# Turning the first of four token pairs by VectorE blocks and DRAM instead of TensorE

## The chip, the cores and the metric

The kernel runs on one core of a Trainium2 chip. The metric is the device time of one execution in microseconds, as a median over several runs. A profiled execution comes with it, in which every instruction of every engine has a start and a duration.

## The reference, cut to what matters

All data are fp32. There are 2048 tokens of 576 features; the two-part layer below is applied twice.

```python
def _A_ref(x, dft_seq_re, dft_seq_im, dft_hid_re, dft_hid_im):
    a = jnp.einsum("bsd,ed->bse", x, dft_hid_re)
    b = jnp.einsum("bsd,ed->bse", x, dft_hid_im)
    y = jnp.einsum("ts,bse->bte", dft_seq_re, a) - jnp.einsum("ts,bse->bte", dft_seq_im, b)
    return y
def _B_ref(x, w1, b1, w2, b2):
    y = _layernorm(x, axis=-1)
    h = _gelu(jnp.einsum("bsd,df->bsf", y, w1) + b1)          # 576 -> 4608
    return jnp.einsum("bsf,fd->bsd", h, w2) + b2              # 4608 -> 576
x = A_x
for _ in range(2):
    x = x + _A_ref(_layernorm(x, axis=-1), ...)
    x = x + _B_ref(_layernorm(x, axis=-1), ...)
```

## The kernel before

Every fp32 product is made of three TensorE passes over two parts of each operand: a high part, rounded to fp32r by ScalarE, and a low part, which is the rest and which VectorE gets by subtracting. The large products are cut into two by two blocks and done with seven block products instead of eight, so block sums of each operand are needed too, and each of the seven operands needs its high and its low part.

A layer has a sequence stage (DFT over tokens), and then, for each half of the 1024 tokens, a *feature phase* (`hidden`, DFT over features, residual, layer norm) and the channel MLP (`mlp`). So there are four feature phases in an execution. The change touches only them.

A feature phase goes through eight tiles of 128 tokens, n = 0 to 7. Tiles 2j and 2j+1 form *pair* j; one comes from the first 512 tokens of the half and one from the second. For tile n, `hidden` does in this order:

- SyncE loads operands two tiles ahead (`h.load(n + 2)`, four DMAs from `uv_mid` and one for the residual).
- `turn(n + 1)` splits the next tile's left operand (ScalarE high, L201; VectorE low, 128x1152).
- `next(ln)` lets the previous tile's layer norm go on: `normalize` (ScalarE, L252) writes the normalized tile n-1 into the pair's block `t8[j]`.
- `rests(j)` (ScalarE, L922), at even n, copies the 32 features that don't fill a block of 128.
- 54 matmuls of 288 columns into a PSUM pair from `space()`, a ring of four.
- in the middle of these (k = 2 of 9), at n = 3 and 5, `turn_sums` makes high and low parts of two single blocks and one more (through `parts`), and then four block differences on VectorE (128x384 each). At k = 4 GpSimd adds the output bias to the residual tile.
- after the matmuls, VectorE adds the result to the residual tile (L195) and makes the statistics of tile n (`stats`: VectorE, then three small GpSimd instructions, L229 to L233).
- at n = 3 and 5, `turn_parts` makes the parts of the four sums (one ScalarE instruction of 1536 elements, two VectorE ones).
- at n = 2, 4 and 6, `turn_blocks(n // 2 - 1)` turns pair j = 0, 1, 2: eight TensorE transposes of 128x128 (L936), four of 96 columns (L939), and two ScalarE copies from PSUM (L940, L941). Pair 3 has a path of its own at the end.

The operand `y` of the MLP has tokens along its free dimension, which is why the normalized tiles are turned at all. The order of instructions on each engine is the order in which the program writes them (`manual_schedule`); an engine doesn't pass an instruction that waits. Two blocks of 2304 columns (`t8s`) hold the pairs in turn: pair 0 and pair 2 have the same one. Nearly all vector and DMA instructions go through helpers, so their lines in the profile are those of the helpers: L192 `dma`, L195 `add`, L198 `sub`, L208 `mm`.

Of the kernel before, what the change touches and what calls it, by code (L numbers as in the profile page):

```python
# [8 lines left out]
F32 = mybir.dt.float32  # L9
F32R = mybir.dt.float32r  # L10
AF = mybir.ActivationFunctionType
# [4 lines left out]
P = 128  # L16
NT = S // P
DH = D // 2
NP = NT // 2
# [138 lines left out]
def spectral_mixer(ctx: ExitStack, tc: tile.TileContext, x, dh, c0, cs, w1, b1, w2, b2, out):  # L158
# [8 lines left out]
    nc = tc.nc  # L167
# [23 lines left out]
    def dma(dst, src):  # L191
        nc.sync.dma_start(dst, src)  # L192

    def add(engine, dst, a, b, op=OP.add):
        engine.tensor_tensor(dst, a, b, op=op)  # L195

    def sub(engine, dst, a, b):
        engine.tensor_tensor(dst, a, b, op=OP.subtract)  # L198

    def split(hi, lo, src):  # L200
        nc.scalar.activation(hi, src, AF.Copy)  # L201
        sub(nc.vector, lo, src, hi.bitcast(F32))
# [4 lines left out]
    def mm(o, a, b, start, stop):  # L207
        nc.tensor.matmul(o, a, b, start=start, stop=stop, skip_group_check=True)  # L208


    def moments():

        t = small.tile([P, 34], F32, name="moments")
        return (t[:, :24].rearrange("p (a b) -> p a b", a=2),
                t[:, 24:].rearrange("p (a b) -> p a b", a=2))

    def stats(src, twice=False, plain=False):


        st, mv = (v[:, 0] for v in moments())  # L220
# [12 lines left out]
        nc.gpsimd.tensor_tensor(mv[:, 4:5], power[:, 2:3], mv[:, 4:5], op=OP.subtract)  # L233
        return mv
# [16 lines left out]
    def normalize(dst, src, mv):  # L251
        nc.scalar.activation(dst, src, AF.Identity, bias=mv[:, 4:5], scale=mv[:, 3:4])  # L252
# [3 lines left out]
    stage, raw = R.alloc(3 * 5 * P, low=True), A.alloc(4 * 3 * P, low=True)  # L256
# [493 lines left out]
    class Hidden:  # L750
# [106 lines left out]
        def turn(self, n, place=None):  # L857
            if n >= NP:
                return
            v = self.uv[n](2 * D)  # L860
            v = (v.bitcast(F32) if self.half else v).rearrange("p (q k t) -> p k q t", q=4, t=32)
            self.ut[n] = place or R.place(UT_AT[self.half][n % 2], 2 * KH * P)
            o = self.ut[n](2, KH, 4, 32)
            split(o[:, 0], o[:, 1], v)
            yield
            self.uvs.give(self.uv.pop(n))

    def drain(*gens):
        gens = list(gens)
        while gens:  # L870
            for g in list(gens):
                if next(g, "end") == "end":
                    gens.remove(g)

    def hidden(h, mlp):

        half, src, order, turn = h.half, h.src, h.order, h.turn
        ring = None

        def space():  # L880
            return pp[ring.pop(0)] if ring else h.space()
# [6 lines left out]
        y = Y(7, 5, TC)  # L888
        t8s = Slots(A, 2, 8 * DH)
        es, b2t = A.alloc(7 * 3 * 32, low=True), A.alloc(D, low=True)  # L890
        dma(b2t(D), b2.to_broadcast([P, D]))
        t8 = {}

        def norms(n):

            if n % 2 == 0:
                t8[n // 2] = t8s.take()
            v = t8[n // 2](8, DH)
            tile_x = xv[:, :, order[n]]
# [4 lines left out]
            if n < NP - 1:  # L904
# [12 lines left out]
            yield  # L917

        def rests(j):
            v = t8[j](8, DH)  # L920
            if j < 3:
                nc.scalar.activation(es(7, 3, 32)[:, :4], v[:, 0:4, None, 2 * P:].to_broadcast([P, 4, 3, 32]), AF.Copy)  # L922
                return
            e = es(7, 3, 32)
            nc.scalar.activation(e[:, :, 1].bitcast(F32R), v[:, 1:8, 2 * P:], AF.Copy)  # L925
            nc.gpsimd.tensor_copy(e[:, :, 0], v[:, 1:8, 2 * P:])
            sub(nc.gpsimd, e[:, :, 2], v[:, 1:8, 2 * P:], e[:, :, 1])
# [12 lines left out]
            nc.scalar.activation(x[:, :, 0:2], a.rearrange("p a (b k t) -> p (a b) k t", k=2, t=P), AF.Copy)  # L940
            nc.scalar.activation(x[:96, :, 2], b[:96, 0].rearrange("p (b t) -> p b t", t=P), AF.Copy)  # L941

        def parts(j, block, i, high=True, low=True, engine=nc.vector):


            x = t8[j](8 * DH)[:, 6 * P:].rearrange("p (b k t) -> p b k t", b=4, k=3)[:, block]
            at = slice(j * P, (j + 1) * P)
            if high:
                nc.scalar.activation(y[:, i, 0:3, at], x, AF.Copy)  # L949
            if low:  # L950
                sub(engine, y[64:96, i, 2, at], x[64:96, :, 2], y[64:96, i, 2, at].bitcast(F32))
                sub(nc.vector, y[:, i, 3:5, at], x[:, :, 0:2], y[:, i, 0:2, at].bitcast(F32))

        def turn_sums(j):
            x = t8[j](8 * DH)[:, 6 * P:].rearrange("p (b k) -> p b k", b=4)
            b11, b12, b22, b21 = (x[:, k] for k in range(4))
            parts(j, slice(2, 4), slice(0, 2))
            parts(j, slice(0, 1), slice(2, 3))
            g = nc.vector
            sub(g, b11, b12, b11)  # L960
            sub(g, b12, b22, b12)
            sub(g, b22, b22, b11)
            sub(g, b21, b21, b22)

        def turn_parts(j):
            parts(j, slice(0, 4), slice(3, 7))
            t8s.give(t8.pop(j))

        def turn_y(j):
            v = t8[j](8, DH)  # L970
# [25 lines left out]
        for n in range(NP):  # L996
            h.load(n + 2)
            for k in (n,) if n < NP - 1 else (n, n + 1):
                h.keep_d(k)
            if n:  # L1000
                drain(turn(n + 1))
                next(ln)
            if n >= 2 and n % 2 == 0:
                rests(n // 2 - 1)
            if n == NP - 3:
                next(mlp)
            o = space()
            if n == NP - 1:

                h.uvs.close()  # L1010
                next(mlp)
                o, ring = pp[3], [2, 3] * 3
            u = h.ut.pop(n)
            for k in range(KH):
                if n == 0 and k == KH // 2:
                    drain(turn(1))
                if n in (3, 5) and k == 2:
                    turn_sums((n - 3) // 2)
                if k == 4:
                    next(ln, None)  # L1020
                for m, (a, b) in enumerate(PASSES):
                    for e in range(2):
                        mm(o[:, e, :DH], u(2, KH, P)[:, a, k], h.dd[k][b](2, DH)[:, e],
                           k == 0 and m == 0, k == KH - 1 and m == 2)
            u.free()
            clock[0] += 1
            tile_x = xv[:, :, order[n]]
            add(nc.vector, tile_x, o[:, :, :DH], tile_x)
            ln = norms(n)
            next(ln)  # L1030
            if n in (3, 5):
                turn_parts((n - 3) // 2)
            if n >= 2 and n % 2 == 0:
                turn_blocks(n // 2 - 1)
            if n == NP - 2:
                turn_sums(2)


# [16 lines left out]
        tile_x = xv[:, :, order[NP - 1]]  # L1055
# [309 lines left out]
    for layer in range(2):  # L1365
        src, to = (xd, out) if layer else (x, xd)
# [64 lines left out]
```

## Time and profile before

| | |
|---|---|
| median of 3 runs | 2670.5 us (2668.57 to 2672.72) |
| the profiled execution | 2675.18 us, of which its span is 2673.3 us |
| granted TensorE clock, mean | 0.998 |
| TensorE matmul busy | 2639.7 us, 99% |
| VectorE busy | 1836.7 us, 69% |
| ScalarE busy | 1105.9 us, 41% |
| GpSimd busy | 814.3 us, 30% |
| the 12 transposes of pair 0 | in the four phases at 403.5, 892.8, 1737.7 and 2212.8 us from the span's start |

A row of the timeline or of the groups gives start and duration in us, engine, line, operation, the tiles written and read, the shape (partitions x elements) and the count; in brackets the idle time of that engine just before, and what ended it. PE is TensorE's matmul, PEld its weight load, which runs ahead of the matmul by about a tenth of a us and shows most clearly when TensorE's queue moves.

### The profile page before, as it was taken

Reading aid. Unit: us, or ns where it says so; the run is one execution under the profiler, and the core shown is the slowest. Engines: PE = TensorE matmul, PEld = TensorE weight load, DVE = VectorE, ACT = ScalarE, POOL = GpSimd, SP = SyncE. Lnnn points to the kernel's source line nnn. Section 1 sums busy time; section 2 is a strip of 40 time slices with the busy share of each in tenths; the row PEclk is TensorE's granted clock in tenths of the full one; section 3 lists DMA queues with packets and bytes.
Section 4 is the critical chain, followed back from the end, with each engine's and each line's share of the span. In section 5 each row is a group of like instructions: output and inputs, shape, how many; then the busy total and the mean of one; then the engine's idle time right before and its main releaser. Section 6 shows DMA issues by size and latency. Waiting matters only on the chain. (4 is left out here: it accounts for less than half of the span.)

```text
span 2673.3 us, 44719 instructions
## 1 busy us (share of the span) xinstructions
PE 2639.7 (99%) x17252; PEld 2472.7 (92%) x17252; DVE 1836.7 (69%) x2547; ACT 1105.9 (41%) x1785; POOL 814.3 (30%) x698
## 2 busy tenths in 40 slices
PE   9999999999999999999999999999999999999998
PEld 9999999888888988998899999998989999899998
DVE  8999987877777665556677767576555557655555
ACT  6555555544453343333344333343333324433332
POOL 6343433444443432223251000132222233322222
PEclk9999999999999999999999999999999999999999
DMA  5677786777778566666553333646666685666664
GB/s 182 238 260 243 239 262 211 259 267 272 267 277 291 173 187 196 193 219 206 154 209 131 122 122 122 202 146 192 195 195 192 193 264 148 203 192 195 193 194 152
DMA packets 223109, 544.90 MB, mean 204 GB/s; under 512 B 23584, under 2 KB 74784, under 8 KB 222752
## 3 DMA queue, kind: packets, MB, share of 16 engines
q1 hardware_dynamic: 209568, 511.94, 60.8%
q10 hardware_dynamic: 13328, 30.09, 2.9%
q8 instruction: 137, 2.24, 0.3%
q14 instruction: 76, 0.62, 0.1%
HBM read 429.87 MB, written 114.72 MB: 204 GB/s over the span
## 5 line engine op out<-in xcount | busy, mean ns | idle before, releaser
L208 PE MATMUL bank<-R 128*128 128x288 f32 (+2 forms) x16972 | 2607.4, 315 | 17.9 <-DVE A L195 7.3
L208 PEld LDWEIGHTS bank<-R 128*128 128x128 f32 x16972 | 2441.0, 189 | 180.1 <-DVE A L195 17.0
L195 DVE TENSOR_TENSOR A<-bank,A 128x576 f32<-128x576 f32 (+3 forms) x808 | 568.8, 710 | 545.2 <-PE bank L208 453.1
L198 POOL TENSOR_TENSOR R<-A,R 128x512 fp32r<-128x512 f32 (+1 forms) x286 | 373.5, 1317 | 904.5 <-ACT R L1240 865.8
L198 DVE TENSOR_TENSOR R<-A,R 128x1024 fp32r<-128x1024 f32 (+10 forms) x539 | 536.0, 1020 | 61.7 <-ACT R L651 25.3
L195 POOL TENSOR_TENSOR A<-A 128x576 f32<-128x576 f32 (+2 forms) x102 | 148.7, 1461 | 537.0 <-ACT A L692 339.8
L1179 ACT ACTIVATE bank<-bank,b1t 128x512 f32<-128x512 f32 (+1 forms) x224 | 144.9, 647 | 369.2 <-DVE bank L195 242.6
L1240 ACT ACTIVATE R<-A 128x512 fp32r<-128x512 f32 x288 | 177.0, 629 | 273.2 <-DVE A L198 123.5
L198 POOL TENSOR_TENSOR A<-A 128x288 f32<-128x288 f32 (+3 forms) x152 | 194.1, 1281 | 222.8 <-DVE R L198 90.3
L195 DVE TENSOR_TENSOR bank<-bank,A 128x512 f32<-128x512 f32 (+1 forms) x228 | 152.3, 670 | 143.5 <-PE bank L208 142.6
L651 ACT ACTIVATE R<-A 128x1024 fp32r<-128x1024 f32 x196 | 206.2, 1053 | 106.0 <-PE bank L208 63.6
L198 DVE TENSOR_TENSOR A<-A 128x1024 f32<-128x1024 f32 (+3 forms) x166 | 160.3, 970 | 6.2
L198 DVE TENSOR_TENSOR R<-bank,R 128x512 fp32r<-128x512 f32 x232 | 156.3, 677 | 4.8 <-ACT R L1240 4.2
L1206 ACT ACTIVATE A<-bank 128x512 f32<-128x512 f32 (+1 forms) x76 | 43.7, 575 | 225.4 <-PE bank L208 225.4
L1240 ACT ACTIVATE R<-bank 128x512 fp32r<-128x512 f32 x216 | 121.2, 595 | 30.4 <-PE bank L208 30.4
L198 DVE TENSOR_TENSOR A<-bank,A 128x512 f32<-128x512 f32 x144 | 98.1, 681 | 0.0
L278 ACT ACTIVATE R<-A 128x256 fp32r<-128x256 f32 x126 | 52.0, 413 | 64.6 <-DMA A<-in_w 29.3
L252 ACT ACTIVATE A<-A,moments 128x576 f32<-128x576 f32 x58 | 48.6, 861 | 71.5 <-POOL moments L233 43.1
L1179 ACT ACTIVATE A<-bank,b1t 128x512 f32<-128x512 f32 (+1 forms) x76 | 50.5, 665 | 66.5 <-DVE bank L195 66.5
L229 POOL TENSOR_TENSOR moments<-moments,power 128x1 f32<-128x1 f32 x32 | 27.5, 860 | 130.1 <-DVE moments L226 130.1
L279 ACT ACTIVATE R<-A,power,middle 128x128 fp32r<-128x128 f32 x126 | 60.8, 483 | 0.0
L949 ACT ACTIVATE R<-A 128x768 fp32r<-128x768 f32 (+2 forms) x36 | 32.9, 947 | 40.2 <-DVE A L198 40.0
(64 smaller groups left out, 631.8 us busy)
## 6 DMA issues: line engine op xcount, KB each, us to landing
R<-w_parts SPq DMA_DIRECT2D x504, 320.0 KB, 3.4
R<-w_parts SPq DMA_DIRECT2D x189, 576.0 KB, 3.7
A<-in_cs SPq DMA_DIRECT2D x112, 512.0 KB, 4.1
w_parts<-R SPq DMA_DIRECT2D x63, 576.0 KB, 5.2
w_parts<-R ACTq DMA_DIRECT2D x81, 320.0 KB, 3.7
uv_mid<-A SPq DMA_DIRECT2D x28, 576.0 KB, 3.0
w_parts<-R SPq DMA_DIRECT2D x45, 320.0 KB, 4.3
A<-in_w SPq DMA_DIRECT2D x72, 192.0 KB, 4.7
```

The costliest lines, as they stand in the source:

```text
L195: engine.tensor_tensor(dst, a, b, op=op)
L198: engine.tensor_tensor(dst, a, b, op=OP.subtract)
L208: nc.tensor.matmul(o, a, b, start=start, stop=stop, skip_group_check=True)
L229: nc.gpsimd.tensor_tensor(mv[:, 3:4], mv[:, 2:3], power[:, 0:1], op=OP.pow)
L252: nc.scalar.activation(dst, src, AF.Identity, bias=mv[:, 4:5], scale=mv[:, 3:4])
L278: nc.scalar.activation(t[:, 1:4:2], src[:, 0:3:2], AF.Copy)
L279: nc.scalar.activation(t[:, 2], src[:, 1], AF.Identity, bias=power[:, 2:3], scale=middle)
L651: nc.scalar.activation(self.cells[t, i](2, NP, P)[:, 0], self.source(t, i), AF.Copy)
L949: nc.scalar.activation(y[:, i, 0:3, at], x, AF.Copy)
L1179: nc.scalar.activation(dst, src, AF.Gelu_apprx_tanh, bias=bias(f))
L1206: nc.scalar.activation(up, o, AF.Copy)
L1240: nc.scalar.activation(H[q, k](2, TC)[:, 0], src, AF.Copy)
```

## The change

Pair 0 is no longer turned by TensorE. Its two normalized tiles are written by ScalarE in another order (three instructions instead of one each, `[g, e, i]` with 32 features i innermost). At n = 2 VectorE transposes all 128x1152 in blocks of 32x32, and SyncE writes the result to a DRAM tensor `y_mid` in two DMAs (the second one four copies of the rest of 32 features). At n = 3, k = 1, four DMAs read it back, each into 32 partitions, so that features lie on partitions. `turned_x` is a part of the block `t8[0]`, as before.

The steps that use it move. Before, pair 0 had `turn_sums` at n = 3 and `turn_parts` at the end of n = 3. Now the first parts and the sums of pair 0 are written at the start of n = 4, behind `rests(1)`, and its sums go to GpSimd; its `turn_parts` is written at the start of n = 5, behind `turn(6)` and ahead of `next(ln)`, that is, ahead of `normalize` of tile 4 into the same block. Its parts take more and smaller instructions, since the turned data have another order. `h.ring += 2` keeps the PSUM ring as it was. Pairs 1, 2 and 3 keep their way.

```diff
+    yd = nc.dram_tensor("y_mid", (P, 4, 3 * P), F32, kind="Internal").ap()
...
+            if n < 2:
+                z = raw().rearrange("p (g e i) -> p e g i", e=4, i=32)
+                z = z[:, 0:4:3] if n == 0 else z[:, 1:3]
...
+            if n < 2:
+                xg = tile_x.rearrange("p e (g i) -> p e g i", i=32)
+                for k in range(2):
+                    normalize(z[:, :, k:8:2], xg[:, :, 4 * k:4 * k + 4], mv)
+                normalize(z[:, :, 8], xg[:, :, 8], mv)
...
+        def raw():
+            return t8[0](8 * DH)[:, :4 * DH]
+        def turned_x():
+            return t8[0](8 * DH)[:, 6 * P:]
+        def write_turned():
+            v = raw()
+            nc.vector.transpose(v, v)
+            dma(yd[:, :, :2 * P], v[:, :8 * P].rearrange("p (c f) -> p c f", c=4))
+            dma(yd[:, :, 2 * P:], v[:, None, 8 * P:].to_broadcast([P, 4, P]))
+        def read_turned():
+            x, src = turned_x().rearrange("p (q f) -> p q f", q=4), yd.rearrange("(q d) c f -> c d q f", q=4)
+            for c in range(4):
+                dma(x[32 * c:32 * c + 32], src[c])
...
-        def parts(j, block, i, high=True, low=True, engine=nc.vector):
+        def parts(j, e, i, high=True, low=True, engine=nc.vector):
+            if j == 0:
+                x = turned_x().rearrange("p (q f e t) -> p f e q t", q=4, f=3, t=32)[:, :, e]
+                yv = y[:, :, :, at].rearrange("p i f (q t) -> p f i q t", q=4)[:, :, i]
+                n = i.stop - i.start
+                highs = [(yv[:, f], x[:, f]) for f in range(3)] if n > 2 else [
+                    (yv[:, 0:3, k], x[:, :, k]) for k in range(n)]
+                lows = [(yv[:, 3 + f], x[:, f], yv[:, f]) for f in range(2)] if n > 2 else [
+                    (yv[:, 3:5, k], x[:, 0:2, k], yv[:, 0:2, k]) for k in range(n)]
+                lows = [tuple(z[64:96] for z in (yv[:, 2], x[:, 2], yv[:, 2])), *lows]
...
-            parts(j, slice(2, 4), slice(0, 2))
-            parts(j, slice(0, 1), slice(2, 3))
-            g = nc.vector
+        def first_parts(j):
+            parts(j, slice(2, 4), slice(0, 2))
+            parts(j, slice(0, 1), slice(2, 3))
+        def turn_sums(j):
+            g = nc.vector if j else nc.gpsimd
             sub(g, b11, b12, b11)
             sub(g, b12, b22, b12)
             sub(g, b22, b22, b11)
             sub(g, b21, b21, b22)
...
             if n:
                 drain(turn(n + 1))
+                if n == 5:
+                    turn_parts(0)
+                    t8.pop(0)
                 next(ln)
-            if n >= 2 and n % 2 == 0:
-                rests(n // 2 - 1)
+            if n == 2:
+                write_turned()
+                h.ring += 2
+            if n == 4:
+                rests(1)
+                first_parts(0)
+                turn_sums(0)
+                t8s.give(t8[0])
+            if n == 6:
+                rests(2)
...
-                if n in (3, 5) and k == 2:
-                    turn_sums((n - 3) // 2)
+                if n == 3 and k == 1:
+                    read_turned()
+                if n == 5 and k == 2:
+                    first_parts(1)
+                    turn_sums(1)
...
-            if n in (3, 5):
-                turn_parts((n - 3) // 2)
-            if n >= 2 and n % 2 == 0:
+            if n == 5:
+                turn_parts(1)
+                t8s.give(t8.pop(1))
+            if n in (4, 6):
                 turn_blocks(n // 2 - 1)
```

More of the change, by code (lines that the diff above doesn't have):

```diff
@@ L941, in turn_blocks @@
             nc.scalar.activation(x[:96, :, 2], b[:96, 0].rearrange("p (b t) -> p b t", t=P), AF.Copy)
-        def parts(j, block, i, high=True, low=True, engine=nc.vector):
-            x = t8[j](8 * DH)[:, 6 * P:].rearrange("p (b k t) -> p b k t", b=4, k=3)[:, block]
+        def parts(j, e, i, high=True, low=True, engine=nc.vector):
             at = slice(j * P, (j + 1) * P)
+            if j == 0:
[7 more added lines that the diff above has]
+                lows = [tuple(z[64:96] for z in (yv[:, 2], x[:, 2], yv[:, 2])), *lows]
+            else:
+                x, yv = t8[j](8 * DH)[:, 6 * P:].rearrange("p (b k t) -> p b k t", b=4, k=3)[:, e], y[:, i, :, at]
+                highs = [(yv[:, :, 0:3], x)]
+                lows = [(yv[64:96, :, 2], x[64:96, :, 2], yv[64:96, :, 2]), (yv[:, :, 3:5], x[:, :, 0:2], yv[:, :, 0:2])]
@@ L948, in parts @@
             if high:
-                nc.scalar.activation(y[:, i, 0:3, at], x, AF.Copy)
+                for dst, src in highs:
+                    nc.scalar.activation(dst, src, AF.Copy)
             if low:
[L951 to L956, printed above, removed]
+                for k, (dst, src, hi) in enumerate(lows):
+                    sub(nc.vector if k else engine, dst, src, hi.bitcast(F32))
@@ L957, in turn_sums @@
+        def first_parts(j):
             parts(j, slice(2, 4), slice(0, 2))
             parts(j, slice(0, 1), slice(2, 3))
-            g = nc.vector
+        def turn_sums(j):
+            x = t8[j](8 * DH)[:, 6 * P:]
+            x = x.rearrange("p (b k) -> p b k", b=4) if j else x.rearrange("p (g e t) -> p e g t", e=4, t=32)
+            b11, b12, b22, b21 = (x[:, k] for k in range(4))
+            g = nc.vector if j else nc.gpsimd
             sub(g, b11, b12, b11)
@@ L966, in turn_parts @@
             parts(j, slice(0, 4), slice(3, 7))
-            t8s.give(t8.pop(j))
         def turn_y(j):
```

3 lines of the change are left out of this document (2 added, 1 removed).

## The prediction

> **What bounds the kernel now.** I read the page first: its engine shares and its chain of work.
>
> ```profile
> PE 2639.7 (99%) x17252; PEld 2472.7 (92%) x17252; DVE 1836.7 (69%) x2547; ACT 1105.9 (41%) x1785; POOL 814.3 (30%) x698
> ...
> PE 15%; DVE 0%; ACT 0%; issue 0%; ACTq 0%
> ```
>
> TensorE is busy for 99% of the span, and nearly all that the chain follows back is TensorE. So a step costs time only where it lengthens TensorE's queue or makes it wait. Next I read TensorE's weight loads in the third feature phase (layer 1, first half; the other three look alike). Columns: start, duration, engine, line, what, count; in brackets the idle time ahead and what ended it.
>
> ```profile
> 1737.73 0.93 PEld L936 LDWEIGHTS bank<-ident,A 128*128 128x128 f32 x8
> 1738.62 0.45 PEld L939 LDWEIGHTS bank<-ident,A 128*96 128x96 f32 x4
> 1739.06 14.42 PEld L208 LDWEIGHTS bank<-R 128*128 128x128 f32 x108
> 1753.42 0.27 PEld L936 LDWEIGHTS bank<-ident,A 128*128 128x128 f32 x2
> 1754.58 0.64 PEld L936 LDWEIGHTS bank<-ident,A 128*128 128x128 f32 x6 [0.89 <-ACT A L252]
> 1755.19 0.45 PEld L939 LDWEIGHTS bank<-ident,A 128*96 128x96 f32 x4
> 1755.63 14.42 PEld L208 LDWEIGHTS bank<-R 128*128 128x128 f32 x108
> 1769.99 0.27 PEld L936 LDWEIGHTS bank<-ident,A 128*128 128x128 f32 x2
> 1771.21 0.64 PEld L936 LDWEIGHTS bank<-ident,A 128*128 128x128 f32 x6 [0.95 <-ACT A L252]
> 1771.82 0.45 PEld L939 LDWEIGHTS bank<-ident,A 128*96 128x96 f32 x4
> 1772.26 2.82 PEld L208 LDWEIGHTS bank<-R 128*128 128x128 f32 x21
> ```
>
> Tiles 3 and 4 take 14.42 us, 7.21 each. The 12 transposes of pair 0 take 1739.06 - 1737.73 = 1.33 us, without a wait. Those of pairs 1 and 2 wait 0.89 and 0.95 us in their midst for the ScalarE normalize of the odd tile (L252). From the end of tile 2 to the start of tile 7 pass 1772.26 - 1737.73 = 34.53 us: this is the stretch to recompute.
>
> **The change part by part.** I count from the end of tile 2 (0 = 1737.73).
>
> *What goes from TensorE.* 12 transposes, 1.33 us a phase. The ScalarE copies L940, L941 and L922 of pair 0 go too; ScalarE is no bound. The 0.89 us of pair 1 also go: tile 3 no longer has pair 0's parts and sums on VectorE ahead of its add, and its normalize (below, 12.9 at the end) comes 1.5 us before TensorE asks for it at 14.42. If TensorE then waited for nothing, tile 7 would start at 4 x 7.21 + 2 x 1.33 = 31.5, which is 3.0 us earlier than now.
>
> *Tiles 0 to 2: normalize, block transpose, write.* The groups by shape and two VectorE rows:
>
> ```profile
> L205 DVE STREAM_TRANSPOSE A<-A 128x1152 f32<-128x1152 f32 x32 | 44.1, 1377 | 2.9
> ...
> L949 ACT ACTIVATE R<-A 128x384 fp32r<-128x384 f32 x12 | 6.1, 510 | 0.0
> ...
> 1730.86 0.76 DVE L195 TENSOR_TENSOR A<-bank,A 128x576 f32<-128x576 f32 x1 [1.97 <-PE bank L208]
> ...
> 1738.06 0.76 DVE L195 TENSOR_TENSOR A<-bank,A 128x576 f32<-128x576 f32 x1 [3.74 <-PE bank L208]
> ```
>
> The transpose has the very shape of L205: 1.38 us, inside the 3.74 us in which VectorE waits for tile 2. The three smaller normalizes cost at most 3 x 0.51 us against 0.87 now, on a ScalarE that no longer copies pair 0 from PSUM. I take nothing for these.
>
> *The DMAs.* SyncE gets two writes (786 KB) and four reads (786 KB) a phase.
>
> ```profile
> uv_mid<-A SPq DMA_DIRECT2D x28, 576.0 KB, 3.0
> ...
> A<-uv_mid SPq DMA_DIRECT2D x64, 144.0 KB, 4.5
> ...
> 1742.97 2.33 SPq L192 DMA_DIRECT2D A<-uv_mid x4
> ```
>
> The nearest write lands in 3.0 us, the nearest reads in 4.5, and four take 2.3 us to issue. Written from about 0.5, landed at about 4.5, read until about 7, landed at about 11.5; first used at 13.4 (below). So hidden, with 2 us to spare; without that cover each us late is a us a phase. Behind the writes on SyncE stands the load of tile 5, behind the waiting reads that of tile 6, wanted at 14.4 at the earliest: these have the room.
>
> *Tile 4: parts and sums of pair 0.* This is what decides. In program order ScalarE has normalize of tile 3, `rests(1)`, then the first parts of pair 0; GpSimd's sums wait for these; at tile 5 ScalarE and VectorE have `turn_parts(0)`, which waits for the sums, and only behind it normalize of tile 4 and all of pair 1's parts.
>
> ```profile
> 1735.31 0.87 ACT L252 ACTIVATE A<-A,moments 128x576 f32<-128x576 f32 x1 [3.08 <-POOL moments L233]
> ...
> 1741.45 0.85 ACT L252 ACTIVATE A<-A,moments 128x576 f32<-128x576 f32 x1
> ...
> L198 DVE TENSOR_TENSOR R<-A,R 32x256 fp32r<-32x256 f32 x1 | 0.4, 417 | 2.2 <-ACT R L949 2.2
> L198 DVE TENSOR_TENSOR R<-A,R 128x256 fp32r<-128x256 f32 x2 | 0.8, 425 | 0.0
> L198 DVE TENSOR_TENSOR R<-A,R 32x128 fp32r<-32x128 f32 x2 | 0.6, 284 | 0.0
> ```
>
> Tile 3 ends at 7.21, its add starts 0.33 later (1738.06 against 1737.73). From the add to the normalize it is 4.45 us where a VectorE split follows the statistics at once (1730.86 to 1735.31), as it will here, and 3.39 where none does (1738.06 to 1741.45). So normalize starts at 12.0 (low end 10.9), ends at 12.9; `rests`, 384 elements like the 0.51 us of L949: 13.4. Three high parts of 384, 0.51 each: 14.95. The lows of the first two blocks start at 14.45 and take 0.42 + 2 x 0.43, those of the third 0.28 + 0.43: done at 16.4 (low end 15.3). Only then may GpSimd overwrite the blocks.
>
> ```profile
> 384.31 1.01 POOL L198 TENSOR_TENSOR A<-A 128x384 f32<-128x384 f32 x1 [5.42 <-DVE R L198]
> L198 POOL TENSOR_TENSOR A<-A 128x384 f32<-128x384 f32 x54 | 79.7, 1477 | 79.4 <-DVE R L198 37.8 <-issue 26.0 <-ACT bank L1179 8.5
> 1741.08 0.19 POOL L233 TENSOR_TENSOR moments<-power,moments 128x1 f32<-128x1 f32 x1
> 1752.44 1.19 POOL L233 TENSOR_TENSOR moments<-power,moments 128x1 f32<-128x1 f32 x1
> L198 DVE TENSOR_TENSOR R<-A,R 128x1152 fp32r<-128x1152 f32 x4 | 5.4, 1356 | 3.8 <-ACT R L201 3.8
> ```
>
> A GpSimd subtraction of this size took 1.01 us alone and 1.48 in the mean beside VectorE. Four in a row: 4.1 to 5.9. Beside them VectorE has only one long subtraction from SBUF, the split of tile 6 (1.36), so I take 4.8: 21.2. The L233 rows show such meetings, 0.19 us alone and 1.19 beside VectorE.
>
> The Trainium skill, "SBUF — State Buffer", section "SBUF: two separate sides", says that a GpSimd instruction and a VectorE one with two SBUF inputs shut each other out for a whole instruction; L233's 1.19 us agrees. By it the sums would end at 16.4 + 4.1 + 1.4 = 21.9, and the total below would be 3 us more.
>
> *Tile 5 on.*
>
> ```profile
> L1240 ACT ACTIVATE R<-A 128x512 fp32r<-128x512 f32 x288 | 177.0, 629 | 273.2 <-DVE A L198 123.5 <-DVE A L195 61.8 <-DVE R L198 44.0
> L198 DVE TENSOR_TENSOR R<-A,R 128x512 fp32r<-128x512 f32 x18 | 13.1, 734 | 0.2
> L198 DVE TENSOR_TENSOR R<-A,R 32x512 fp32r<-32x512 f32 x8 | 5.5, 683 | 0.2
> 1758.02 0.86 ACT L252 ACTIVATE A<-A,moments 128x576 f32<-128x576 f32 x1
> ```
>
> `turn_parts(0)`: three highs of 512, 1.9 us: 23.1. The first low needs the last high; three lows, 0.68 + 2 x 0.73 = 2.15: 25.3. Normalize of tile 4 overwrites the block that these read, so it starts at 25.3. From there the kernel's order is as before: pair 1's parts, its sums on VectorE, the add and statistics of tile 5, normalize of tile 5, ten transposes of pair 2. Before, this took from 1758.02 to 1772.26, 14.24 us without a hole on that path. So tile 7 starts at 39.5 instead of 34.53: 5.0 us later a phase, though TensorE has less to do. It stands idle for about 39.5 - 31.5 = 8.0 us within the transposes of pair 2. Ends: sums begun at 15.3 and taking 4.1 give +3.2; sums of 5.9 and a round trip 2 us late give about +8.
>
> *The clock.* An idle time this long is in the trace only at its end (windows from the span's start), and a cold start only at its beginning (TensorE's group of the stretch from 1.3 to 6.3 us).
>
> ```profile
> 2666.00:2667.00 1.00, 0.02 (x1) 0.00 (x0) 0.76 (x1) 0.00 (x0) 0.00 (x0) 1.00 1.03 361
> ...
> 2669.00:2669.50 0.50, 0.00 (x0) 0.00 (x0) 0.00 (x0) 0.00 (x0) 0.00 (x0) 0.50 1.09 383
> L1358 PE MATMUL bank<-ident 128*128 128x128 f32 x23 | 5.2, 424 | 1.3 <-POOL ident masks.py:199 1.3
> ```
>
> The granted clock (the third number from the end) is 0.50 three us after the last matmul. At the start 23 transposes took 5.2 us, while the 12 of pair 0 take 1.33, so 23 would take 2.5. An idle of 8 us should lose the clock, and getting it back costs about what it did there, 5.2 - 2.5 = 2.7, which I take. Bounds: 0 (no fall) and 2.7.
>
> The Trainium skill, "TensorE: Matmul & The Clock Gate", Part 1, puts the return at one busy window of about 3.4 us. By it 1.7 would be lost instead of 2.7, and the total would be 4 us less.
>
> *Sum.* 4 x (5.0 + 2.7) = 31 us on the profiled execution's 2675.2, which is 4.7 above the median: 2706 there, 2701 as a median.
>
> **The rivals.** *The stall without the clock's fall*: 4 x 5.0 = 20, so 2690. For it speaks that no phase of the trace has shown a fall; against it the end rows.
>
> *Faster: the way over GpSimd is hidden.* Place: `turn_parts(0)` at tile 5. If the sums were done when ScalarE reaches it, normalize of tile 4 would start as now, pair 2 would keep its 0.95 us wait, and 1.33 + 0.89 = 2.2 us a phase would be gained: 2662. It decides at sums ending by 14; break-even is normalize of tile 4 at 34.53 - 14.24 = 20.3, sums ending at 16.2. Against it: the first parts end at 16.4 by rows, and four GpSimd subtractions can't take less than 4. It needs an error in my reading of the order.
>
> *The round trip is late*: if reads land after 13.4, every us adds one: 3 us late makes 2713.
>
> **How the numbers follow.** 0.2%, about 5.3 us, is what a measurement of this kernel can tell from no change. Stall with clock loss 0.57 (2701), without 0.20 (2690), late round trip 0.07 (2713): slower 0.84. Hidden 0.10: faster. Gains and stall about equal 0.06: same. The range runs from the low end without a clock loss, 2670.5 + 4 x 3.2 = 2683, a little widened to 2680, to the high end, 2670.5 + 4 x (8 + 2.7) = 2713, taken as 2715.
>
> **What would show it.** Right: no L936 before tile 3; no wait within pair 1's transposes; four GpSimd 128x384 between tiles 4 and 5 of a phase; ScalarE waiting for them ahead of three 128x512 instructions; about 8 us idle in TensorE ahead of pair 2's transposes, ended by L252; granted clock under 1 behind it. Wrong: pair 2's wait stays near 1 us, or normalize of tile 4 comes before `turn_parts(0)` is through.

## The result, and the profile after

The changed kernel takes 2696.79 us (median of 4, 2695.08 to 2698.12) beside 2671.24 us for the kernel before in the same comparison (2668.57 to 2672.72): a ratio of 1.0099, 95% interval 1.0084 to 1.0113. It is 25.6 us slower. Its profiled execution took 2698.12 us, with a span of 2696.3 and a mean granted clock of 0.992.

In the changed kernel `normalize` is L253, `sub` L199, `mm` L209, the turning of pairs 1 and 2 L962 and L965, and the high parts L988. From its page, engine shares, and from its list of waits (us in total, times, longest):

```profile
PE 2639.1 (98%) x17204; PEld 2473.8 (92%) x17204; DVE 1827.3 (68%) x2543; ACT 1105.5 (41%) x1801; POOL 833.0 (31%) x714
...
PEld bank L962 <- ACT A L253: 34.3, 4, 9.4
```

TensorE, VectorE and ScalarE have no more work than before, and GpSimd has 19 us more; TensorE waits. Its weight loads in the third feature phase, to be laid beside those of before, with the row at which the MLP goes on (1807.61), and the two rows of before that follow those shown in the prediction:

```profile
1760.13 0.93 PEld L962 LDWEIGHTS bank<-ident,A 128*128 128x128 f32 x8
1761.03 0.45 PEld L965 LDWEIGHTS bank<-ident,A 128*96 128x96 f32 x4
1761.46 14.42 PEld L209 LDWEIGHTS bank<-R 128*128 128x128 f32 x108
1775.83 0.27 PEld L962 LDWEIGHTS bank<-ident,A 128*128 128x128 f32 x2
1785.52 1.14 PEld L962 LDWEIGHTS bank<-ident,A 128*128 128x128 f32 x6 [9.42 <-ACT A L253]
1786.64 0.84 PEld L965 LDWEIGHTS bank<-ident,A 128*96 128x96 f32 x4
1787.49 13.29 PEld L209 LDWEIGHTS bank<-R 128*128 128x128 f32 x89
...
1807.61 2.57 PEld L209 LDWEIGHTS bank<-R 128*128 128x128 f32 x21 [0.58 <-ACT A L1263]
```

```profile
1783.65 0.77 PEld L980 LDWEIGHTS bank<-ident,A 128*128 128x128 f32 x6
...
1790.80 76.58 PEld L208 LDWEIGHTS bank<-R 128*128 128x128 f32 x435 [0.57 <-ACT A L1206]
```

There is no wait at pair 1 and one of 9.42 us at pair 2. Tiles 3 and 4 take 14.36 us from start to start, so tile 2 ended at 1760.13 - 14.36 = 1745.77. From there to the MLP's step it is 61.84 us, and before 1790.80 - 1737.73 = 53.07. The difference, piece by piece: pair 2's wait +8.47; its ten remaining transposes at a lower clock 1.97 for 1.05, +0.92; tile 7 and the matmuls behind it (89 loads) 13.24 for 11.39, +1.85; pair 0's transposes -1.33; pair 1's wait -0.88; pair 3's steps -0.27: +8.76, which is the difference but for rounding. The same difference is 6.0, 6.4, 8.8 and 7.5 us in the four phases, 28.7 in all. The span grew by 23.0; the stretches outside the phases were 5.7 us shorter.

The granted clock (third number from the end) in and behind the wait:

```profile
1776.00:1779.00 3.00, 0.34 (x3) 0.10 (x1) 2.77 (x7) 0.00 (x0) 0.00 (x0) 1.00 0.68 211
1779.00:1782.00 3.00, 0.00 (x0) 0.00 (x0) 2.87 (x7) 2.54 (x2) 0.63 (x1) 0.89 0.30 117
1782.00:1787.00 5.00, 1.48 (x7) 1.48 (x8) 4.35 (x8) 1.39 (x2) 3.87 (x5) 0.50 0.00 2
1787.00:1792.00 5.00, 5.00 (x25) 4.97 (x24) 2.39 (x4) 3.52 (x5) 2.05 (x4) 0.54 0.00 0
```

It falls to 0.50 within the wait and stays there for some us of work behind it. The steps that lead to the wait, ScalarE, then VectorE and GpSimd:

```profile
1756.51 0.87 ACT L253 ACTIVATE A<-A,moments 128x576 f32<-128x576 f32 x1 [0.17 <-POOL moments L234]
...
1760.57 1.35 ACT L988 ACTIVATE R<-A 128x384 fp32r<-128x384 f32 x3 [2.63 <-DMA A<-y_mid]
...
1768.91 1.67 ACT L988 ACTIVATE R<-A 128x512 fp32r<-128x512 f32 x3 [4.55 <-POOL A L199]
1772.80 0.87 ACT L253 ACTIVATE A<-A,moments 128x576 f32<-128x576 f32 x1 [2.21 <-DVE R L199]
...
1784.60 0.87 ACT L253 ACTIVATE A<-A,moments 128x576 f32<-128x576 f32 x1 [2.69 <-POOL moments L234]
...
1761.54 1.93 DVE L199 TENSOR_TENSOR R<-A,R 32x256 fp32r<-32x256 f32 x5 [3.79 <-ACT R L988]
...
1765.54 1.38 DVE L199 TENSOR_TENSOR R<-A,R 128x1152 fp32r<-128x1152 f32 x1
1770.69 1.99 DVE L199 TENSOR_TENSOR R<-A,R 32x512 fp32r<-32x512 f32 x3 [3.77 <-ACT R L988]
...
1763.60 5.29 POOL L199 TENSOR_TENSOR A<-A 128x384 f32<-128x384 f32 x4 [7.12 <-DMA A<-uv_mid]
```

The steps follow each other: first parts (which waited for the reads from `y_mid`), GpSimd's sums, `turn_parts(0)`, `normalize` of tile 4 (1772.80), and 11.8 us later `normalize` of tile 5 (1784.60), for which TensorE waits. The bracket of GpSimd's sums names a DMA, but in all four phases they begin 0.13 us after VectorE's last first part (here 1761.54 + 1.93 = 1763.47).

### The profile page after: what moved, and what is told of

Read it like the earlier page. It is cut to its first block, busy times and chain, and to the rows that moved or that the text cites. A ratio compares the mean times of both kernels' runs of the same rounds, so it can differ in the third digit from the quotient of the medians.

```text
span 2696.3 us, 44700 instructions
## 1 busy us (share of the span) xinstructions
PE 2639.1 (98%) x17204; PEld 2473.8 (92%) x17204; DVE 1827.3 (68%) x2543; ACT 1105.5 (41%) x1801; POOL 833.0 (31%) x714
## 4 chain that ended last, share of the span: by engine, by line
PE 59%; DVE 2%; DMA 1%; ACT 1%; POOL 1%; issue 1%; SPq 0%; ACTq 0%; DVEq 0%; POOLq 0%
PE bank L209 58%; DVE R L199 1%; DMA R<-dh_parts 0%; POOL A L199 0%; DVE A L199 0%; SPq L193 0%; DMA A<-uv_mid 0%; DVE A L196 0%; DMA A<-y_mid 0%; ACT R L988 0%; ACT A L253 0%; DMA R<-w_parts 0%; DMA A<-x_mid 0%; DVE bank L196 0%; POOL moments L230 0%
## 5 line engine op out<-in xcount | busy, mean ns | idle before, releaser
L209 PE MATMUL bank<-R 128*128 128x288 f32 (+2 forms) x16972 | 2609.3, 315 | 14.5 <-DVE A L196 4.7
L209 PEld LDWEIGHTS bank<-R 128*128 128x128 f32 x16972 | 2443.5, 189 | 177.2 <-DVE A L196 16.8
L199 POOL TENSOR_TENSOR R<-A,R 128x512 fp32r<-128x512 f32 (+1 forms) x286 | 373.5, 1316 | 904.7 <-ACT R L1297 874.9
L199 DVE TENSOR_TENSOR R<-A,R 128x1024 fp32r<-128x1024 f32 (+10 forms) x547 | 530.4, 996 | 94.3 <-ACT R L988 48.4
L199 POOL TENSOR_TENSOR A<-A 128x288 f32<-128x288 f32 (+3 forms) x168 | 212.3, 1267 | 242.0 <-DVE R L199 93.2
L199 DVE TENSOR_TENSOR R<-bank,R 128x512 fp32r<-128x512 f32 x232 | 156.3, 676 | 4.8 <-ACT R L1297 4.2
L199 DVE TENSOR_TENSOR A<-A 128x1024 f32<-128x1024 f32 (+3 forms) x150 | 150.8, 1011 | 5.2
L199 DVE TENSOR_TENSOR A<-bank,A 128x512 f32<-128x512 f32 x144 | 98.0, 681 | 0.0
L253 ACT ACTIVATE A<-A,moments 128x576 f32<-128x576 f32 (+2 forms) x74 | 53.1, 757 | 93.5 <-POOL moments L234 56.2
L230 POOL TENSOR_TENSOR moments<-moments,power 128x1 f32<-128x1 f32 x32 | 31.5, 983 | 115.2 <-DVE moments L227 115.2
L988 ACT ACTIVATE R<-A 128x384 fp32r<-128x384 f32 (+3 forms) x48 | 33.9, 754 | 38.4 <-DVE A L199 18.2
```

Source lines behind the costliest of these rows:

```text
L988: nc.scalar.activation(dst, src, AF.Copy)
```

## The experiments

The theory is the prediction's: pair 0's way over GpSimd ahead of `normalize` of tile 4 makes TensorE wait at pair 2, and the wait costs clock on top. Its rivals were the DRAM round trip, and a stall without the clock's fall. Then the question was why nothing is left when the stall is taken away. For each kernel: its median, and its ratio to the kernel before in the same comparison with the 95% interval. The line numbers of a step differ a little from kernel to kernel.

**The sums on VectorE (`vector_sums`).** After, with

```diff
-            g = nc.vector if j else nc.gpsimd
+            g = nc.vector
```

> Only the engine of pair 0's four sums is changed, from GpSimd to VectorE. Theory (a chain: first parts, sums, parts of the sums, normalize of tile 4, pair 1, normalize of tile 5): the sums take 4 x 0.56 = 2.3 us instead of 5.3, but VectorE's lows of turn_parts(0) then stand behind the add, the statistics and the split of tile 6, so that normalize of tile 4 comes about 1.7 us earlier and TensorE's wait at pair 2 shrinks from 8.6 to about 7 us: 2690. Rival 1, GpSimd alone is the cause: the wait falls to about 1 us and the time to 2671 or less. Rival 2, the DRAM round trip is the cause: no change, 2697.

2689.35 us, 1.0077 (1.0062 to 1.0092). List of waits:

```profile
PEld bank L962 <- ACT A L253: 26.4, 4, 7.0
```

The waits lose 7.9 us, and the time 5.9 by the ratios (1.0099 - 1.0077; the intervals overlap a little) or 7.4 by the medians. Not all of this is GpSimd's: in the profiled execution of after ScalarE waited 4.0 us in all for the reads from `y_mid`, and here 0.4. Beside the kernel without the round trip (below), where nothing waits for reads, the waits are 31.5 - 26.4 = 5.1 us shorter. So GpSimd's slowness is part of the stall, but about a sixth of it only.

**TensorE kept busy in the wait (`warm`).** After, with 64 transposes into an unused bank behind the first two of pair 2:

```diff
                                         v[:, e, k * P:(k + 1) * P], ident)
+                if j == 2 and n == 0:
+                    for _ in range(64):
+                        nc.tensor.transpose(b[:, 1, :P], ident, ident)
```

> 64 transposes of the identity into an unused part of PSUM stand within pair 2's transposes, where TensorE waits, so that it is busy for about 6.8 us of the 8.6 (each phase); nothing else is changed. Theory (the wait costs its length and the lost clock besides): the granted clock stays at 1.00, the ten transposes behind the wait take 1.05 instead of 1.97 us and tile 7 runs at full speed, together about 2 us a phase: 2689. Rival 1, tile 7's half speed is made up by a shorter wait later: only the 0.9 us of the transposes are gained, 2693. Rival 2, the clock has no price here: 2697 or more.

2687.06 us, 1.0068 (1.0053 to 1.0083); mean granted clock 0.999 where after had 0.992. That is 8.3 us less than after by the ratios, 9.7 by the medians, 2.1 to 2.4 us a phase. The lists of waits, for the reads from `y_mid` in after and here, and for `normalize` of tile 5 here:

```profile
ACT R L988 <- DMA A<-y_mid: 4.0, 3, 2.6
...
ACT R L991 <- DMA A<-y_mid: 0.5, 1, 0.5
...
PEld bank L962 <- ACT A L253: 3.6, 4, 1.0
```

The 64 transposes and the wait that is left fill 7.9 us a phase, as long as the wait of after where its reads weren't late (7.87 us, first phase): the chain of steps is unchanged. In the traces the four phases are 10.5 us shorter than in after. Of this 2.8 are ahead of `normalize` of tile 5, since the reads were nearly in time here; the other 7.7 are work behind the wait, 1.6, 1.5, 2.6 and 2.0 us in the four phases. So the price of the lost clock is 1.9 us a phase by the traces, and 2.1 to 2.4 by the times, a part of which may be the reads.

**No round trip (`no_round_trip`).** After without its DMAs:

```diff
-            dma(yd[:, :, :2 * P], v[:, :8 * P].rearrange("p (c f) -> p c f", c=4))
-            dma(yd[:, :, 2 * P:], v[:, None, 8 * P:].to_broadcast([P, 4, P]))
...
-                if n == 3 and k == 1:
-                    read_turned()
```

> The two writes and four reads through DRAM are left out (pair 0's operand is then old data; VectorE's block transpose stays). Theory: the round trip only costs what the first parts of pair 0 waited for the reads, 0, 0.3, 2.6 and 1.1 us in the four phases, 4 us in all, since everything behind moves with them: 2693. Rival, the round trip and its traffic are the cause of the loss: 2671 or less.

2695.27 us, 1.0102 (1.0087 to 1.0117).

```profile
PEld bank L960 <- ACT A L253: 31.5, 4, 7.9
```

The waits lose 2.8 us, and the four phases of the trace are 4.0 us shorter together (0.3, 0.3, 2.3 and 1.1), as expected; the time can't be told from that of after. The DMAs are not the cause of the stall.

**Pair 0's transposes alone (`no_turn`).** Before without them, the rests and the copies from PSUM:

```diff
-            if n >= 2 and n % 2 == 0:
+            if n == 2:
+                h.ring += 2
+            if n >= 4 and n % 2 == 0:
                 rests(n // 2 - 1)
...
-            if n >= 2 and n % 2 == 0:
+            if n >= 4 and n % 2 == 0:
                 turn_blocks(n // 2 - 1)
```

> The kernel before, with pair 0's twelve transposes, its rests and the two copies from PSUM left out and nothing in their place (pair 0's operand is then old data); sums and parts stay where they were. It is the most that taking the transposes away can give by itself. Theory: 1.33 us a phase go, pair 1's wait stays at 0.9 to 1.2 us since VectorE still has pair 0's sums ahead of tile 3's add: 2671 - 5 = 2666. Rival 1, these transposes were hidden: 2671. Rival 2, pair 1's wait goes too: 2662.

2673.18 us, 1.0014 (1.0004 to 1.0023): a miss, since 1.33 us of TensorE a phase went and nothing was gained. Third phase, rows of TensorE, VectorE, ScalarE and GpSimd, and a window:

```profile
1754.84 0.64 PEld L936 LDWEIGHTS bank<-ident,A 128*128 128x128 f32 x6 [2.74 <-ACT A L252]
...
1756.08 15.78 PEld L208 LDWEIGHTS bank<-R 128*128 128x128 f32 x108
...
1737.75 0.76 DVE L195 TENSOR_TENSOR A<-bank,A 128x576 f32<-128x576 f32 x1 [3.74 <-PE bank L208]
...
1739.85 1.36 DVE L198 TENSOR_TENSOR R<-A,R 128x1152 fp32r<-128x1152 f32 x1
...
1748.58 0.75 DVE L195 TENSOR_TENSOR A<-bank,A 128x576 f32<-128x576 f32 x1
...
1742.19 0.87 ACT L252 ACTIVATE A<-A,moments 128x576 f32<-128x576 f32 x1 [3.48 <-POOL moments L233]
...
1739.88 1.74 POOL L229 TENSOR_TENSOR moments<-moments,power 128x1 f32<-128x1 f32 x1 [2.51 <-DVE moments L226]
...
1756.00:1759.00 3.00, 3.00 (x15) 2.99 (x14) 0.60 (x1) 3.00 (x4) 1.16 (x4) 0.50 1.01 278
```

And the same two places of before, the add of tile 3 and GpSimd's instruction:

```profile
1748.32 0.75 DVE L195 TENSOR_TENSOR A<-bank,A 128x576 f32<-128x576 f32 x1
...
1740.18 0.55 POOL L229 TENSOR_TENSOR moments<-moments,power 128x1 f32<-128x1 f32 x1 [2.50 <-DVE moments L226]
```

In before, ScalarE's copies of pair 0 from PSUM hold up the split of tile 4, so that the statistics of tile 2 pass GpSimd first (0.55 us) and its `normalize` starts 3.39 us after the add. Without the copies VectorE's split starts at 1739.85, at the same time as L229, which takes 1.74 instead; `normalize` comes 1742.19 - 1737.75 = 4.44 us after the add. All of pair 0's parts and sums stand behind it on VectorE, and behind these the add of tile 3. So pair 1's wait grew from 0.89 to 2.74 us, which takes the 1.33 back and more, and the clock fell behind the wait: the next 108 loads took 15.78 us instead of 14.42. Over the four phases the waits at pairs 1 and 2 grew from 7.6 to 12.5 us, and the work behind three of the four waits at pair 1 took 1.6, 1.6 and 1.3 us longer: 4.9 + 4.5 us against the 5.3 us of the transposes. The Trainium skill, "SBUF — State Buffer", section "SBUF: two separate sides", says that a VectorE instruction with two SBUF inputs and a GpSimd one shut each other out for a whole instruction; L229, begun 0.03 us behind the split and ended 0.41 us behind its end, agrees.

**The two waits of before taken away (`late_sums`).** Before, with the four sums of pairs 0 and 1 behind the add and the statistics of tiles 3 and 5, and their parts (`turn_parts`) one tile later:

```diff
                 if n in (3, 5) and k == 2:
-                    turn_sums((n - 3) // 2)
+                    first_parts((n - 3) // 2)
...
             if n in (3, 5):
-                turn_parts((n - 3) // 2)
+                turn_sums((n - 3) // 2)
...
+            if n in (4, 6):
+                turn_parts(n // 2 - 2)
```

> The kernel before, TensorE transposes and all; only VectorE's order is changed: at tiles 3 and 5 the four sums of pairs 0 and 1 stand behind the tile's add and statistics instead of ahead of them, and the parts of the sums behind the next tile's split. Theory (pairs 1 and 2 wait because VectorE has a pair's sums ahead of the odd tile's add): both waits of 0.9 us go, 1.84 us a phase, 2670 - 7 = 2663. Rival 1 (VectorE is so full that the work pushed back delays the next tile's split or normalize): the waits move, 2670. Rival 2 (the waits come from GpSimd's statistics, which meet VectorE's long subtractions either way): 2668 to 2670.

2670.03 us, 0.9993 (0.9985 to 1.0002): a miss. From the list of waits of before, then from that of this run and its third phase:

```profile
PEld bank L936 <- ACT A L252: 7.6, 8, 1.0
...
PEld bank L982 <- DVE A L198: 8.0, 12, 1.7
...
1770.69 3.53 DVE L198 TENSOR_TENSOR A<-A 128x384 f32<-128x384 f32 x4
1774.13 0.75 DVE L195 TENSOR_TENSOR A<-bank,A 128x576 f32<-128x576 f32 x1
```

The 7.6 us of waits at pairs 1 and 2 (L936) are gone, and 8.0 us have come up at pair 3 (L982): there VectorE's sums of pair 2 stand ahead of the add of tile 7. The same without pair 0's transposes (`late_sums_no_turn`):

> The same order, and pair 0's twelve transposes, its rests and the two copies from PSUM left out besides (pair 0's operand is then old data). Theory (in the kernel before these transposes cost nothing because TensorE waits for VectorE's chain anyway; once that chain is short they cost their 1.33 us): 4 x 1.33 = 5 us less than the run with the transposes, about 2658. Rival (TensorE's queue isn't what is saved, or the chain takes it up again): the same as the run with them.

2669.72 us, 0.9991 (0.9982 to 1.0). The waits at pair 3 grew from 8.0 to 11.1 us, and 1.2 us came back at L936: together 4.3 of the 5.3 us saved. Behind two of the four long waits at pair 3 (2.58 to 2.69 us) the clock fell, too.

**The changed kernel's chain opened (`unlinked`).** After, with pair 2's tiles in swapped places of their block (so that `normalize` of tile 4 doesn't overwrite what `turn_parts(0)` reads), the sums on GpSimd behind that `normalize`, and `turn_parts(0)` behind tile 5's statistics:

```diff
-            z = v[:, 2:4] if n % 2 == 0 else v[:, 0:2]
+            z = v[:, 2:4] if (n % 2 == 0) != (n // 2 == 2) else v[:, 0:2]
...
                 if n == 5:
-                    turn_parts(0)
-                    t8.pop(0)
+                    turn_sums(0)
...
                 first_parts(0)
-                turn_sums(0)
...
             if n == 5:
+                turn_parts(0)
+                t8.pop(0)
                 turn_parts(1)
```

> The changed kernel with the link to normalize of tile 4 cut: pair 2's tiles change places in their block, so that tile 4 isn't written over what pair 0's parts read; GpSimd's sums of pair 0 stand behind tile 4's statistics and its parts behind tile 5's statistics. Theory (the wait is what stands ahead of normalize of tile 4): normalize of tile 4 at about 22 instead of 27 us after tile 2's end, pair 1's work then beside the sums on GpSimd and up to 3 us slower, TensorE's wait 8.6 down to 4 to 6 us: 2683, between 2678 and 2690. Rival 1 (the sums' length is what counts, wherever they stand): 2695. Rival 2 (the order alone is the cause): 2665 or less.

2685.07 us, 1.0051 (1.0037 to 1.0064).

```profile
PEld bank L963 <- ACT A L253: 19.5, 4, 6.1
```

That is 12.8 us less than after by the ratios, 11.7 by the medians: the part of the chain through `turn_parts(0)`. In the third phase `normalize` of tile 4 comes 20.6 us after the end of tile 2 instead of 27.0, but from there to `normalize` of tile 5 13.0 us pass instead of 11.8. The work that stands there on VectorE is pair 0's and pair 1's. Next, that was spread too (`spread`): pair 0's first parts at the end of tile 4, pair 1's sums and parts at tile 6.

```diff
+            if n == 4:
+                first_parts(0)
...
             if n == 6:
                 rests(2)
+                turn_sums(1)
+                turn_parts(1)
```

> The changed kernel with pair 0's and pair 1's VectorE work spread behind the adds and statistics of tiles 4, 5 and 6: pair 0's first parts behind tile 4's statistics, its sums on GpSimd behind tile 4's normalize, its parts behind tile 5's statistics; pair 1's sums and parts behind tile 6's split. Theory: TensorE's wait at pair 2 falls to about 1 us and 1.33 + 0.89 us a phase are gained there, but VectorE then is about 4 us behind when the MLP begins, which costs that much: 2670, between 2660 and 2682. Rival (a round trip that comes at 14 us leaves VectorE enough room behind): 2661.

2684.11 us, 1.0048 (1.0034 to 1.0062): a miss. Pair 2's wait is down to 3.0 us, and the waiting has moved to pair 3 and, in part, to the MLP's first steps (8.1 us there instead of 3.2).

```profile
PEld bank L1022 <- DVE A L199: 15.7, 8, 3.8
PEld bank L963 <- ACT A L253: 3.0, 4, 0.8
```

**Room on VectorE at pair 3.** In `late_sums`, `late_sums` without the transposes, and `spread`, the sums of pair 2 went to GpSimd (`pool_sums`, `pool_sums_no_turn`, `spread_pool_sums`):

```diff
-            g = nc.vector
+            g = nc.gpsimd if j == 2 else nc.vector
```

> late_sums with the four sums of pair 2 (at n = 6) on GpSimd instead of VectorE. Theory: VectorE's queue sets the end of the phase. In late_sums these four sums held the add of tile 7 until 1774.13 in the third phase, though its matmuls were done about two us earlier, and TensorE then waited in pair 3's transposes, 8.0 us in 12 waits over the four phases. With the sums on GpSimd (four at 1.0 to 1.3 us, done before its three small instructions of tile 7) the add comes at once and these 8 us go: 2670 - 8 = 2662 (2658 to 2667). Rival: TensorE's waits are again only moved, now to the four high parts of pair 2 or to pair 3's own steps: within 2 us of late_sums, 2668 to 2672.

> pool_sums without pair 0's transposes, its rests and its copies from PSUM: pair 0 of y is then made from data that were never turned. Theory: the 1.33 us of these transposes are worth their face only where VectorE leaves room. late_sums_no_turn gained nothing over late_sums, its waits at pair 3 grew from 8.0 to 11.1; with the sums of pair 2 off VectorE both should go: 4 x 1.33 = 5.3 us under pool_sums, about 2657 (2652 to 2662). Rival: VectorE's or ScalarE's remaining work still sets the end, and it equals pool_sums within 2 us.

> spread with the sums of pair 2 on GpSimd too. It is the changed kernel's way (pair 0 by VectorE blocks and DRAM) with its sums off the path. In spread TensorE waited 15.7 us in 8 for VectorE in pair 3's transposes. Theory as for pool_sums: these go, 2684 - 16 = 2668 (2664 to 2675), still not under pool_sums_no_turn. Rival: VectorE is behind by more than these sums (pair 1's sums and parts also lie in tile 6), and half or more stays: 2676 to 2684.

2670.62 us, 0.9996 (0.9987 to 1.0005); 2670.24, 0.9999 (0.999 to 1.0008); 2683.54, 1.0044 (1.0031 to 1.0056): three misses. `pool_sums`, its list of waits and its third phase (VectorE, then GpSimd):

```profile
PEld bank L982 <- DVE A L198: 8.2, 12, 1.7
...
1772.96 0.76 DVE L195 TENSOR_TENSOR A<-bank,A 128x576 f32<-128x576 f32 x1 [1.71 <-PE bank L208]
...
1777.65 0.58 DVE L907 TENSOR_SCALAR A<-A,moments 128x576 f32<-128x576 f32 x1 [2.23 <-POOL moments L229]
...
1771.42 4.29 POOL L198 TENSOR_TENSOR A<-A 128x384 f32<-128x384 f32 x4 [0.56 <-DVE R L198]
1775.67 1.44 POOL L195 TENSOR_TENSOR A<-A 128x576 f32<-128x576 f32 x1
1777.08 0.54 POOL L229 TENSOR_TENSOR moments<-moments,power 128x1 f32<-128x1 f32 x1
```

VectorE now adds tile 7 as soon as TensorE gives it. But the next step, the scale of tile 7 (L229), stands on GpSimd behind the sums and an output bias, and TensorE waits as long as before. It is the same in `spread_pool_sums`: VectorE waits 4.02 us for this step in the third phase, and TensorE's waits at pair 3 are 15.4 us in 4 instead of 15.7 in 8. Last, that bias behind L229 (`pool_sums_order`):

```diff
-                if k == 4:
+                if k == 4 and n < NP - 1:
                     next(ln, None)
...
-            ln = norms(n)
+            bias, ln = ln, norms(n)
             next(ln)
+            if n == NP - 1:
+                next(bias)
```

> pool_sums with tile 6's output bias (GpSimd, 1.44 us) moved behind the one small GpSimd instruction of tile 7's statistics. In pool_sums the add of tile 7 came at once (1772.96, for TensorE), but that small instruction stood on GpSimd behind the four sums (4.29 us, to 1775.7) and this bias, and began at 1777.08; VectorE waited 2.23 us for it and TensorE again 8.2 us in pair 3's transposes. Theory: the wait is that of one queue at a time, and with the bias behind, the instruction begins at about 1775.7, 1.4 us earlier a phase: 4 x 1.4 = 5.6, 2670.6 - 5.6 = 2665 (2662 to 2668). Rival: the wait turns up at once at the next place of the phase (the step behind it, pair 3's last transposes or the MLP's first ones): 2669 to 2672.

2669.38 us, 0.9995 (0.9985 to 1.0006): a miss.

```profile
PEld bank L982 <- DVE A L198: 7.0, 12, 1.4
...
1774.84 1.41 POOL L195 TENSOR_TENSOR A<-A 128x576 f32<-128x576 f32 x1
...
1774.91 1.67 DVE L907 TENSOR_SCALAR A<-A,moments 128x576 f32<-128x576 f32 x1 [0.80 <-POOL moments L229]
```

The add of tile 7 stands at 1771.64 in this run, so L229 began 2.7 us after it instead of 4.1. But now the bias meets VectorE's L907, which takes 1.67 us instead of 0.58. Of the 1.4 us a phase, 0.3 reach TensorE ((8.2 - 7.0) / 4). No version beat the kernel before by more than can be measured.

## Why the prediction was right, step by step

It gave 2701 us with the stall and the clock's fall as the likeliest case; 2696.8 was measured. In the third phase, counted from the end of tile 2 (1745.77):

| step | predicted | measured |
|---|---|---|
| `normalize` of tile 3 | 12.0 | 10.7 |
| first parts of pair 0 begin | 13.4 | 14.8 |
| first parts done | 16.4 | 17.7 |
| GpSimd's four sums | 4.8 | 5.3 |
| `normalize` of tile 4 | 25.3 | 27.0 |
| from there to tile 7 | 14.24 | 14.69 |
| TensorE idle in pair 2's transposes, mean of four | 8.0 | 8.6 |
| loss by the clock, mean of four (by `warm`) | 2.7 | 1.9 by the traces, 2.1 to 2.4 by the times |
| a whole phase, mean of four | +7.7 | +7.2 |

In the other three phases `normalize` of tile 3 came at 11.7 to 11.9, the first parts began at 13.3 to 14.2, and `normalize` of tile 4 came at 25.5 to 26.5, nearer to the prediction.

*The chain was right.* The order on ScalarE, the sums as its middle, the place of the wait and its length came out as read from the program order and the rows of before. `unlinked` shows that this order is the cause of a good part, 12 to 13 us.

*The clock was right and a little large.* `warm` gives 7.7 to 9.7 us for what the prediction put at 10.8 (the lower figure that it names, 1.7 us a phase, comes nearest by the traces), and the rival without a fall (2690) is refuted: the clock fell in all four phases.

*The round trip was not hidden with 2 us to spare.* In the third phase ScalarE waited 2.63 us for it, in the others 0, 0.3 and 1.1. The prediction took nothing for the three small normalizes and put the block transpose into VectorE's wait for tile 2. In the third phase the transpose began only at the end of tile 2, behind the last of these normalizes, and held the add of tile 2 until 1.4 us after that end instead of 0.33; the writes were issued from 1.5 us instead of 0.5. The reads, issued until 8.3 instead of 7, then landed 6.5 us later instead of 4.5. And `normalize` of tile 3 came early, since the split of tile 5 waited 2.76 us for its own load and the statistics passed GpSimd ahead of it. The step that failed is the cover of the DMAs. Its price, a us for each us late, isn't refuted: the 4.0 us that ScalarE waited in all go with 2.8 us more of TensorE's waits and 4.0 us of the phases in the traces, and the times of the two kernels can't tell.

*The gain side was taken for granted.* The prediction subtracted 1.33 us for pair 0's transposes from the phase. Where there is a stall this only lengthens the stall, so the total isn't touched. But `no_turn` shows that the kernel before can't use the 1.33 us in its own order: the statistics of tile 2 run into VectorE's split and the wait at pair 1 grows. And the gain of the rival that forecast 2662 was never seen: in `spread`, where pair 2 waits only 3.0 us in all, the time is still 2684, because the waiting comes up behind. What a way over GpSimd that is hidden by itself would give is not shown. In the `late_sums` and `pool_sums` pairs, too, the kernel without the transposes was no faster, with its waits at pair 3 3 to 4 us longer.

*The sum was in part luck.* Of the 31 us predicted 20 were for the stall and 10.8 for the clock. Of the 28.7 us that came in the phases, `warm` leaves 18.2 for the stall without a lost clock, 7.7 are the clock's, and 2.8 are TensorE's longer waits for late reads, which the prediction put at nothing. So both terms were somewhat large, and the late reads made up for about half of that. The stretches outside the phases were 5.7 us shorter than in the profiled execution of before, 2.3 of them ahead of the first phase. That execution took 3.9 us more than the median of before (2671.24), and the one of after 1.3 more than its own, so part of this is chance between executions; the rest wasn't traced.

What stays open: whether pair 0's transposes could be cashed in by an order in which no chain of ScalarE, VectorE and GpSimd steps ends later than TensorE. Three other orders were tried on the kernel before, and in each the wait turned up at another place: VectorE's sums, GpSimd's queue, the two engines on each other.

## What to carry to other kernels

A TensorE at 99% doesn't mean that an instruction taken from it is time gained. Follow the chain of the other engines to the next thing TensorE waits for; if that chain doesn't get shorter, the wait grows by what was saved. And ask of removed work what it kept apart: here the PSUM copies of pair 0 held a split behind the statistics that it would have collided with.

Work whose input arrives later falls into a stretch that has work of its own, and the order written into strict queues then makes everything behind it late.

A wait of a few us on TensorE can cost more than itself: add the clock that it may lose, here 1.3 to 2.6 us behind a wait.

## What the runs showed of the hardware that had not been expected

An idle time as short as 2.74 us cost the clock: in `no_turn` the granted clock was 0.50 from 1756 to 1759, after TensorE was back at work, and 108 loads took 15.78 us. But a wait of this length doesn't always cost it. The second phase of `no_turn` (108 loads at full speed behind 2.90 us), then the fourth of `late_sums_no_turn` (12 loads, which take 1.6 us where the clock doesn't fall):

```profile
910.91 0.64 PEld L936 LDWEIGHTS bank<-ident,A 128*128 128x128 f32 x6 [2.90 <-ACT A L252]
...
911.96 14.41 PEld L208 LDWEIGHTS bank<-R 128*128 128x128 f32 x108
...
2250.72 2.42 PEld L982 LDWEIGHTS bank<-ident,A 128*128 128x128 f32 x12 [2.61 <-DVE A L198]
```

The three runs without pair 0's transposes have twelve waits of 2.6 to 2.9 us, four each, at pair 1 or pair 3. Behind six of them, the shortest 2.61 us, the mean granted clock of the next 3 us was 0.50 to 0.69; behind the other six, the longest 2.90 us, it was 1.00. So the length alone doesn't decide it, and what does isn't shown. The Trainium skill, "TensorE: Matmul & The Clock Gate", Part 1, names an idle window of about 3.4 us; these waits were shorter, and the measurement decides.

Behind the long wait the work lost 0.92 + 1.85 = 2.8 us in the third phase, as much as about 5.5 us at half speed would lose.

GpSimd and VectorE met on the path, though GpSimd is busy for only 30% of the span and VectorE for 69%: L229 took 1.74 us instead of 0.55 beside a split, L907 1.67 instead of 0.58 beside a bias. TensorE waited for each of them.
